# Moving four reloads behind semaphore waits, and five filler products to two, in a one-core transformer block

## The chip, the core and the metric

The kernel runs on one core of one Trainium2 chip. The metric is device time in microseconds (us), the median of several executions. All engines of the core work from their own instruction streams and meet through semaphores: PE (TensorE, matrix products), DVE (VectorE), ACT (ScalarE), POOL (GpSimd), and SP (SyncE), which issues nearly all DMA transfers of this kernel, in order.

## The reference

A block with adaptive layer norm, linear attention and a gated feed-forward network, on x of 2048 rows by 1024 columns in bf16. `phi(t)` is `t + 1` where t is positive and `exp(t)` elsewhere, plus 1e-6.

```python
mod = (silu(c) @ w_mod).reshape(1, 6, 1, -1)          # w_mod: 1024 x 6144
sa, ca, ga, sb, cb, gb = (mod[:, i] for i in range(6))

h = layernorm(x) * (1 + ca) + sa                      # x: 1 x 2048 x 1024
q, k, v = split_heads(h @ wqkv)                       # 32 heads of 32
pq, pk = phi(q), phi(k)
kv = einsum('bhsd,bhse->bhde', pk, v)
z  = sum over s of pk
o  = (pq @ kv) / (pq @ z + 1e-6)
x  = x + ga * (merge_heads(o) @ wo)

h = layernorm(x) * (1 + cb) + sb
x = x + gb * ((silu(h @ w_gate) * (h @ w_up)) @ w_down)   # 1024 -> 3584 -> 1024
```

## The kernel before

Every instruction is written out in Python in program order through a small recorder, `_Prog`. It notes which bytes of SBUF and which PSUM banks each operation reads and writes and derives the semaphore waits from that; each engine then gets its operations in the order in which they were recorded. Because of the recorder nearly all instructions bear one source line in the profile, L176, and are told apart by the names of their tiles. The order of the work is the order of the Python calls; there is no planner. `P.wait_for(engine, ops)` (line 195) records no operation, only a wait of that engine for the given ones.

SBUF is one arena with offsets given by hand, and tiles share places over time. Three places matter here. `XRES` holds x, 16 tiles of 128 rows (`st` 0 to 15); layer norm overwrites it in place, so x must be loaded a second time before the first residual addition. `STGX[0]` and `STGX[1]` (2 MB each) take column blocks of `w_mod`; both lie where `RB`, the reciprocals of the denominators, lay before. `AT`, used in the feed-forward part, lies over both later.

The stages, in order:

1. The start (lines 398 to 650). x tiles 0 to 3, then the `w_mod` columns of the first scale (`WCA`) and of the first shift (`WSA`), and `wqkv` are loaded on SP's queue. PE transposes the normalised x tiles and computes the scale as columns (`mod_sc(WCA, ...)`: weight load of a 128 x 128 piece of `WCA`, product with one column of `silu(c)`). Between them stand filler products, `warm(n)`: 128 x 128 by 128 x 512, with operands `IDENT` and `E1`, whose result in a PSUM bank is not read. Here are 13 before the transposes of tile 0, and more between these transposes and the first scale columns.
2. Products for q and k over four chunks of 512 rows (`q_phase_chunk0`, `k_group`, `chunk`). Side work such as layer norms and the multiply-accumulate of a `w_mod` block (`macc`, on DVE) is hung into them.
3. The loop over g (line 1005): 16 groups of 16 products, `pk` against the normalised x in `XRES`, giving G, from which kv follows as `WV^T G`, head by head. That last product is `kvt_mm(half)` (line 962), 128 small products of 32 columns. `m_mm(half, nh, banks)` (line 972) multiplies kv by `wo` in 16 products of 32 x 32 by 512 and copies four banks to `MW`, two with ACT and two with DVE.
4. Output of attention and residual (line 1083): for each `st` and each half `nh` of 512 columns `wo_part(st, nh, hgs)` (line 992) makes products of `PQT` with `MW`, and `wo_res(st, nh)` (line 998) adds the PSUM result to `XRES` on DVE. Four PSUM banks (`WO_BANKS`) are used in turn. For tiles 0 and 1 the first four of eight products of each half are done earlier, between `kvt_mm(1)` and `m_mm(1, ...)`; the rest follows in the order (0,0), (1,0) for st = 0 and (0,1), (1,1) for st = 1. The same loop holds the second layer norm of tiles 0 to 3 and `macc` with `STGX[0]`, whose result `MHL` is transposed by a DMA into `MHLT`.
5. Feed-forward over four chunks of 512 rows (line 1107), with weights streamed by `gu_load`. `macc` with `STGX[1]` is in its first chunk.

The reloads are issued on SP around the end of the g loop: `stgx1` (into `STGX[0]`) at g = 10; after the loop `stgx2` (into `STGX[1]`), then four reloads of 256 KB for tiles 0 to 3 of `XRES` (`xr0` to `xr3`), then, after the calls of `m_mm(1, 1, ...)`, three reloads of 1 MB for tiles 4 to 7, 8 to 11 and 12 to 15 (`xr4` to `xr6`). SP meets nothing but the waits of these transfers themselves: `stgx2` for the last reader of `RB`, the `XRES` reloads for PE's reads in the last group.

Of the kernel before, what the change touches and what calls it, by code (L numbers as in the profile page):

```python
# [9 lines left out]
ALU = mybir.AluOpType  # L10
# [252 lines left out]
def bass_adaLN_cond__linear_attn_block__swiglu_ffn__prompt_kernel(  # L263
# [16 lines left out]
    NCH = 4  # L280
# [5 lines left out]
    with ExitStack() as es:  # L286
# [6 lines left out]
        def T(name, off, shape, dt):  # L293
            n = 1
            for s_ in shape[1:]:
                n *= s_
            assert off % 32 == 0 and off + n * mybir.dt.size(dt) <= ARENA, (name, off, shape)
            return nc.alloc_sbuf_tensor_at(name, shape, dt, offset=base + off)

        KB = 1024  # L300
        XRES = T("xres", 0, [128, NST, D], BF16)
# [30 lines left out]
        SUMXH = T("sumxh", SM + 2816, [128, NST, 2], FP32)  # L332
# [17 lines left out]
        STGX = [T("stgx%d" % i, (72 + 16 * i) * KB, [128, NDT, D], BF16) for i in range(2)]  # L350
# [28 lines left out]
        PS = nc.alloc_psum_tensor("ps", [128, 8, 512], FP32)  # L379
# [5 lines left out]
        xv = A_x[0].rearrange("(t p) d -> p t d", p=128)  # L385
# [6 lines left out]
        wmv = w_mod.rearrange("(kt p) n -> p kt n", p=128)  # L392
        cv8 = c.rearrange("o (kt p) -> (o kt) p", p=128)

        P = _Prog()
# [57 lines left out]
        def warm(n=1, bank=2):  # L453
            for _ in range(n):
                P.pe("matmul", out=PS[:, bank, :], lhsT=IDENT[:], rhs=E1[:, 0, :], start=True, stop=True)
# [142 lines left out]
        def act_var(st):  # L598
            P.dve("scalar_tensor_tensor", out=MV[:, st, 1:2], in0=SUMX[:, st:st + 1], scalar=SUMX[:, st:st + 1],
                  in1=SUMSQ[:, st:st + 1], op0=ALU.mult, op1=ALU.subtract)  # L600
            P.dve("tensor_scalar", out=VE[:, st:st + 1], in0=MV[:, st, 1:2], scalar1=-1.0, scalar2=EPS, op0=ALU.mult,
                  op1=ALU.add)
# [7 lines left out]
        def tile_transposes(*js):  # L610
            for dt in range(NDT):
                for j in js:
                    c = (dt % 2) * 512 + j * 128
                    P.pe("transpose", out=PSB[:, 4 + dt // 2, c:c + 128], in_=XRES[:, j, dt * 128:(dt + 1) * 128],
                         identity=IDENT[:])
# [3 lines left out]
        for f in s0_:  # L619
# [3 lines left out]
        s2_[1]()  # L623
        act_xn(0, MV[:, 0, 0:1])
        tile_transposes(0)
        warm(5, bank=3)
        act_var(1)
        P.pool("tensor_tensor", out=RSTD[:, 1:2], in0=VE[:, 1:2], in1=NEGHALF[:, 0:1], op=ALU.pow)
        P.pool("tensor_scalar", out=NMR[:, 1:2], in0=SUMX[:, 1:2], scalar1=RSTD[:, 1:2], scalar2=-1.0,
               op0=ALU.mult, op1=ALU.mult)  # L630
# [80 lines left out]
        def macc(src, kt):  # L711
            if kt == 0:
                P.dve("tensor_scalar", out=ACC[:], in0=src[:, kt, :], scalar1=SILUF[:, kt:kt + 1], scalar2=None,
                      op0=ALU.mult)
            else:
                P.dve("scalar_tensor_tensor", out=ACC[:], in0=src[:, kt, :], scalar=SILUF[:, kt:kt + 1], in1=ACC[:],
                      op0=ALU.mult, op1=ALU.add)

        def macc_split():
            P.dve("tensor_copy", out=MHL[:, 0, :], in_=ACC[:])  # L720
            P.dve("tensor_tensor", out=MHL[:, 1, :], in0=ACC[:], in1=MHL[:, 0, :], op=ALU.subtract)
            xbar(MHLT[:], MHL[:].rearrange("p i d -> p (i d)"))

        def mod_red():
            P.dve("tensor_reduce", out=RED[:], in_=MHLT[:].rearrange("d (i m) p -> d m i p", i=2),
                  axis=mybir.AxisListType.XY, op=ALU.add)

        def mod_fin_col(idx, plus_one):
            P.dve("tensor_copy", out=MODTMP[:, 0:8], in_=RED[:])
            if plus_one:  # L730
                P.dve("tensor_scalar", out=MODTMP[:, 0:8], in0=MODTMP[:, 0:8], scalar1=1.0, scalar2=None,
                      op0=ALU.add)
            P.dve("tensor_copy", out=MODCOL[:, idx, :], in_=MODTMP[:, 0:8])
# [186 lines left out]
        def g_evac(g):  # L920
            h, dt = g // NDT, g % NDT
            bank = G_BANKS[1 if g == 14 else g % 5]
            i = g % 2
            P.act("activation", out=GTMP[:, i, :], in_=ZB[:, h * 512:(h + 1) * 512], func=ACT.Copy,
                  scale=MODCOL[:, 1, dt:dt + 1])
            P.dve("scalar_tensor_tensor", out=G[:, dt, h * 512:(h + 1) * 512], in0=PS[:, bank, :],
                  scalar=MODCOL[:, 0, dt:dt + 1], in1=GTMP[:, i, :], op0=ALU.mult, op1=ALU.add)
# [44 lines left out]
        def m_mm(half, nh, banks):  # L972
            for k in range(4):
                for g in range(4):
                    h = (g + k) % 4
                    P.pe("matmul", out=PS[32 * h:32 * h + 32, banks[g], :],
                         lhsT=KVT[32 * g:32 * g + 32, half, 32 * h:32 * h + 32],
                         rhs=WO[32 * g:32 * g + 32, 4 * half + h, nh * 512:(nh + 1) * 512], start=True, stop=True,
                         skip_group_check=True)
            for g in range(4):  # L980
                dst = MW[:, 4 * half + g, nh * 512:(nh + 1) * 512]
                if g % 2 == 0:
                    P.act("activation", out=dst, in_=PS[:, banks[g], :], func=ACT.Copy)
                else:
                    P.dve("tensor_copy", out=dst, in_=PS[:, banks[g], :])
# [6 lines left out]
        def wo_part(st, nh, hgs):  # L992
            bank = WO_BANKS[(2 * st + nh) % 4]
            for hg in hgs:
                P.pe("matmul", out=PS[:, bank, :], lhsT=PQT[:, hg, st * 128:(st + 1) * 128],
                     rhs=MW[:, hg, nh * 512:(nh + 1) * 512], start=(hg == 0), stop=(hg == NHG - 1))

        def wo_res(st, nh):
            bank = WO_BANKS[(2 * st + nh) % 4]
            xs = XRES[:, st, nh * 512:(nh + 1) * 512]  # L1000
            P.dve("scalar_tensor_tensor", out=xs, in0=PS[:, bank, :], scalar=1.0, in1=xs, op0=ALU.mult,
                  op1=ALU.add, accum_out=SUMXH[:, st, nh:nh + 1])

        ev = 0
        for g in range(16):
# [21 lines left out]
            if g == 10:  # L1027
                P.dma("stgx1", STGX[0][:], wmv[:, :, 3072:4096])
        g_evac(15)
        P.dma("stgx2", STGX[1][:], wmv[:, :, 5120:6144])  # L1030
        for st in range(4):
            P.dma("xr%d" % st, XRES[:, st, :], xv[:, st, :])
        wo_part(0, 0, range(4))
# [5 lines left out]
        wo_part(1, 0, range(1, 4))  # L1039
        wo_part(1, 1, range(4))  # L1040
        m_mm(1, 1, [4, 5, 7, 6])
        for ch in range(1, NCH):
            P.dma("xr%d" % (3 + ch), XRES[:, 4 * ch:4 * ch + 4, :], xv[:, 4 * ch:4 * ch + 4, :])

        def ln2_rstd(ch):
            sl = slice(4 * ch, 4 * ch + 4)
# [8 lines left out]
        def ln2_xn(st):  # L1055
            P.dve("tensor_scalar", out=XN2[:, :, st % 4, :], in0=XRES[:, st, :].rearrange("p (dt q) -> p dt q", q=128),
                  scalar1=MEAN2[:, st:st + 1], scalar2=RSTD2[:, st:st + 1], op0=ALU.subtract, op1=ALU.mult)

        def th2_dma():
            xbar(H2T[:].rearrange("p dt (j s) -> p (dt j) s", j=4), XN2[:].rearrange("p dt j q -> p (dt j q)"))  # L1060

        def th2_mod():
            for dt in range(NDT):
                P.pool("tensor_scalar", out=H2T[:, dt, :], in0=H2T[:, dt, :], scalar1=MODCOL[:, 2, dt:dt + 1],
                       scalar2=MODCOL[:, 3, dt:dt + 1], op0=ALU.mult, op1=ALU.add)

        def ln2_sq(st):
            P.act("activation", out=JUNK[:], in_=XRES[:, st, :], func=ACT.Square, accum_out=SUMSQ[:, st:st + 1])
            if st % 4 == 3:
                ln2_rstd(st // 4)  # L1070
# [12 lines left out]
        for st in range(NST):  # L1083
            for (sw, nh) in (((0, 0), (1, 0)), ((0, 1), (1, 1)))[st] if st < 2 else ((st, 0), (st, 1)):
                wo_part(sw, nh, range(4, 8) if st < 2 else range(8))
                wo_res(sw, nh)
            if st >= 1:
                ln2_sq(st - 1)
            for kt in ((), (0,), (1,), (2, 3), (4,), (5,), (6, 7))[st] if st < 7 else ():
                macc(STGX[0], kt)  # L1090
            if st == 6:
                macc_split()
            if st == 8:
                mod_red()
                mod_fin_col(3, False)
            if st == 7:
                for jj in range(4):
                    ln2_xn(jj)
                th2_dma()
            if st == 8:  # L1100
                th2_mod()
            if st == 7:
                for q in range(4):
                    gu_load(q)
        ln2_sq(NST - 1)
        out_ops = []
        for ch in range(NCH):
            nxt = ch + 1 if ch + 1 < NCH else None
            for ft in range(NFT):
# [27 lines left out]
                if nxt is None and ft in (8, 12):  # L1137
# [3 lines left out]
                          in1=GB_B[:, 896:1024].unsqueeze(1).to_broadcast([128, f1 - f0, 128]), op=ALU.mult)  # L1141
# [5 lines left out]
            for j in range(4):  # L1147
                st = 4 * ch + j
# [7 lines left out]
                for nh in range(2):  # L1156
                    i = nh
                    parts = [(0, 384, bb + 1), (384, 512, 4)] if last and nh == 1 else [(0, 512, bb + nh)]
                    for (c0, c1, pb) in parts:
# [5 lines left out]
                        xs = XRES[:, st, nh * 512 + c0:nh * 512 + c1]  # L1165
# [45 lines left out]
```

## Time and profile before

| what | value |
|---|---|
| median of 10 executions | 830.33 us (829.62 to 831.01) |
| profiled execution: own time | 829.62 us |
| profiled execution: span from first to last instruction | 827.9 us |
| PE busy | 816.5 us, 99% of the span |
| DVE, ACT, POOL busy | 310.6, 197.4, 40.6 us |
| granted TensorE clock | 1.000 |
| `xres` reloads of 1 MB, issue to landing | 13.6 us (median) |
| `out`, 128 KB, issue to landing | 1.7 us (median) |

The span leaves about 1.7 us of the execution's own time outside. A group line of the timeline gives start, time and count of like instructions, and in brackets how long the engine was idle before them and what ended it. "issue" stands where no semaphore explains the idle time. PEld are PE's weight loads, which run beside its products. In the DMA views q1 is the queue of ordinary transfers, q8 and q14 bring instructions.

### The profile page before, as it was taken

Reading aid. Unit: us, or ns where it says so; the run is one execution under the profiler, and the core shown is the slowest. Engines: PE = TensorE matmul, PEld = TensorE weight load, DVE = VectorE, ACT = ScalarE, POOL = GpSimd, SP = SyncE. Lnnn points to the kernel's source line nnn. Section 1 sums busy time; section 2 is a strip of 40 time slices with the busy share of each in tenths; the row PEclk is TensorE's granted clock in tenths of the full one; section 3 lists DMA queues with packets and bytes.
Section 4 is the critical chain, followed back from the end, with each engine's and each line's share of the span. In section 5 each row is a group of like instructions: output and inputs, shape, how many; then the busy total and the mean of one; then the engine's idle time right before and its main releaser. Section 6 shows DMA issues by size and latency. Waiting matters only on the chain.

```text
span 827.9 us, 10429 instructions
## 1 busy us (share of the span) xinstructions
PE 816.5 (99%) x4244; PEld 376.3 (45%) x4323; DVE 310.6 (38%) x664; ACT 197.4 (24%) x336; POOL 40.6 (5%) x59
## 2 busy tenths in 40 slices
PE   8999999999999999999999999999999999999998
PEld 4544444444444444444444444444444444444444
DVE  5797997476955521111221112122111111221111
ACT  4757643123242111011111101111110111111011
POOL 1010000000130000030000003000000300000000
DMA  9969656866397995700455571045557004553000
GB/s 319 289 151 231 149 159 158 183 185 257 68 261 229 290 253 155 181 27 20 129 151 151 154 178 32 19 125 156 151 152 187 26 16 127 152 152 89 0 26 26
DMA packets 199360, 119.32 MB, mean 144 GB/s; under 512 B 57992, under 2 KB 183056, under 8 KB 199312
## 3 DMA queue, kind: packets, MB, share of 16 engines
q1 hardware_dynamic: 199296, 118.65, 53.3%
q8 instruction: 34, 0.56, 0.3%
q14 instruction: 14, 0.11, 0.0%
q10 hardware_dynamic: 16, 0.00, 0.0%
HBM read 100.67 MB, written 4.33 MB: 127 GB/s over the span
## 4 chain that ended last, share of the span: by engine, by line
PE 97%; DVE 1%; issue 1%; DMA 0%; ACT 0%; DVEq 0%; ACTq 0%
PE ps L176 97%; DVE acc L176 1%; DVE pkt L176 0%; DMA cs<-in_c_dram 0%; DVE e L176 0%; DVE pqt L176 0%; ACT e L176 0%; DVE xres L176 0%; DVE ht L176 0%; DVEq L247 0%; ACTq L247 0%
## 5 line engine op out<-in xcount | busy, mean ns | idle before, releaser
L176 PE MATMUL ps<-h2t,gug 128*128 128x512 bf16 x878 | 210.1, 379 | 0.9
L176 PE MATMUL ps<-h2t,guu 128*128 128x512 bf16 x878 | 209.9, 379 | 0.9
L176 DVE TENSOR_TENSOR at<-sg,ps 128x512 bf16<-128x512 bf16 x112 | 77.0, 687 | 282.8 <-PE ps L176 270.6
L176 ACT ACTIVATE sg<-ps 128x512 bf16<-128x512 f32 x112 | 66.9, 597 | 309.7 <-PE ps L176 298.3
L176 PEld LDWEIGHTS ps<-h2t,guu 128*128 128x128 bf16 x896 | 87.7, 98 | 105.7
L176 PEld LDWEIGHTS ps<-h2t,gug 128*128 128x128 bf16 x896 | 87.6, 98 | 105.5
L176 PE MATMUL ps<-wd_a,at 128*128 128x512 bf16 (+1 forms) x502 | 111.9, 377 | 0.5
L176 PE MATMUL ps<-ht,wqk 128*128 128x512 bf16 x499 | 110.3, 379 | 1.0 <-issue 0.2
L176 PE MATMUL ps<-wd_b,at 128*128 128x512 bf16 (+1 forms) x377 | 84.6, 377 | 0.4
L176 PEld LDWEIGHTS ps<-wd_a,at 128*128 128x128 bf16 x512 | 50.1, 98 | 59.7
L176 DVE TENSOR_TENSOR ut<-att,gb_b 128x512 bf16<-128x512 bf16 (+1 forms) x32 | 13.7, 429 | 167.5 <-ACT att L176 167.5
L176 PEld LDWEIGHTS ps<-ht,wqk 128*128 128x128 bf16 x512 | 49.5, 98 | 58.8 <-DVE ht L176 0.4
L176 ACT ACTIVATE att<-ps 128x512 bf16<-128x512 f32 (+1 forms) x32 | 17.4, 591 | 182.1 <-PE ps L176 182.1
L176 PEld LDWEIGHTS ps<-wd_b,at 128*128 128x128 bf16 x384 | 37.6, 98 | 44.6
L176 PE MATMUL ps<-mw,pqt 128*128 128x512 bf16 x249 | 55.6, 379 | 1.9 <-issue 1.6
L176 PE MATMUL ps<-pk,xres 128*128 128x512 bf16 x250 | 55.4, 379 | 0.6 <-issue 0.5
L176 POOL TENSOR_SCALAR h2t<-h2t,modcol 128x512 bf16<-128x512 bf16 x32 | 26.3, 839 | 383.1 <-DMA h2t<-xn 383.1
L176 ACT ACTIVATE e<-ps 128x512 bf16<-128x512 f32 x56 | 33.2, 604 | 31.7 <-PE ps L176 20.7
L176 PEld LDWEIGHTS ps<-mw,pqt 128*128 128x128 bf16 x256 | 24.7, 98 | 31.8 <-issue 2.2
L176 PEld LDWEIGHTS ps<-pk,xres 128*128 128x128 bf16 x256 | 24.7, 98 | 30.0 <-issue 0.9
L176 ACT ACTIVATE junk<-xres 128x1024 bf16<-128x1024 bf16 x24 | 25.4, 1058 | 36.1 <-DVE xres L176 35.8
L176 DVE SCALAR_TENSOR_TENSOR xres<-ps,xres 128x512 bf16<-128x512 f32 x32 | 21.5, 689 | 13.4 <-PE ps L176 13.2
(107 smaller groups left out, 337.6 us busy)
## 6 DMA issues: line engine op xcount, KB each, us to landing
gug<-in_B_w_gate_dram SPq DMA_DIRECT2D x56, 512.0 KB, 3.9
guu<-in_B_w_up_dram SPq DMA_DIRECT2D x56, 512.0 KB, 5.2
xres<-in_A_x_dram SPq DMA_DIRECT2D x20, 256.0 KB, 7.6
rb<-recip_den SPq DMA_DIRECT2D x8, 512.0 KB, 11.5
stgx<-in_w_mod_dram SPq DMA_DIRECT2D x2, 2048.0 KB, 8.4
wd_a<-in_B_w_down_dram SPq DMA_DIRECT2D x4, 1024.0 KB, 7.3
out_dram<-xres SPq DMA_DIRECT2D x31, 128.0 KB, 1.7
xres<-in_A_x_dram SPq DMA_DIRECT2D x3, 1024.0 KB, 13.6
```

Of the source, the lines that this page charges most:

```text
L176: return getattr(e, method)(**kw)
```

## The change

Two things change. First, `warm(5)` ahead of the first scale columns becomes `warm(2)`. Second, four transfers are taken from their places at the end of the g loop and after `m_mm(1, 1, ...)` and issued within the loop over `st`: after the residuals recorded for st = 0, 1 and 2 SP waits for the last of them and issues `xr4`, `xr5` and `xr6` in turn, and after those of st = 3 `stgx2`. `wo_res` returns its operation so that SP can wait for it. On SP the order becomes `stgx1`, `xr0` to `xr3`, `xr4`, `xr5`, `xr6`, `stgx2`, then the transpose of `MHL` as before. On PE three products and their three weight loads leave the stream; DVE, ACT and POOL keep their instructions and order.

```diff
         tile_transposes(0)
-        warm(5, bank=3)
+        warm(2, bank=3)
         act_var(1)
...
         def wo_res(st, nh):
...
-            P.dve("scalar_tensor_tensor", out=xs, in0=PS[:, bank, :], scalar=1.0, in1=xs, op0=ALU.mult,
-                  op1=ALU.add, accum_out=SUMXH[:, st, nh:nh + 1])
+            return P.dve("scalar_tensor_tensor", out=xs, in0=PS[:, bank, :], scalar=1.0, in1=xs, op0=ALU.mult,
+                         op1=ALU.add, accum_out=SUMXH[:, st, nh:nh + 1])
...
         g_evac(15)
-        P.dma("stgx2", STGX[1][:], wmv[:, :, 5120:6144])
         for st in range(4):
             P.dma("xr%d" % st, XRES[:, st, :], xv[:, st, :])
...
         m_mm(1, 1, [4, 5, 7, 6])
-        for ch in range(1, NCH):
-            P.dma("xr%d" % (3 + ch), XRES[:, 4 * ch:4 * ch + 4, :], xv[:, 4 * ch:4 * ch + 4, :])
...
         for st in range(NST):
             for (sw, nh) in (((0, 0), (1, 0)), ((0, 1), (1, 1)))[st] if st < 2 else ((st, 0), (st, 1)):
                 wo_part(sw, nh, range(4, 8) if st < 2 else range(8))
-                wo_res(sw, nh)
+                done = wo_res(sw, nh)
+            if st < 4:
+                P.wait_for("sp", [done])
+                if st < 3:
+                    ch = st + 1
+                    P.dma("xr%d" % (3 + ch), XRES[:, 4 * ch:4 * ch + 4, :], xv[:, 4 * ch:4 * ch + 4, :])
+                else:
+                    P.dma("stgx2", STGX[1][:], wmv[:, :, 5120:6144])
```

## The prediction

> **What bounds the kernel now.** I read the page first: busy time, then the chain that ended last.
>
> ```profile
> span 827.9 us, 10429 instructions
> ...
> PE 816.5 (99%) x4244; PEld 376.3 (45%) x4323; DVE 310.6 (38%) x664; ACT 197.4 (24%) x336; POOL 40.6 (5%) x59
> ...
> PE 97%; DVE 1%; issue 1%; DMA 0%; ACT 0%; DVEq 0%; ACTq 0%
> ```
>
> PE is the bound. A change off PE can gain only where PE sits idle, so the second view is what PE waited for, over the whole span.
>
> ```profile
> PE ps L176 <- DMA cs<-in_c_dram: 2.9, 1, 2.9
> PE ps L176 <- issue: 2.4, 6, 1.5
> ```
>
> 2.9 us pass before the first product and are not touched. The rest is 2.4 us of "issue", which is idle time with no semaphore behind it, and 1.5 of it is one gap. The third view, PE's timeline near the reloads, shows where it lies.
>
> ```profile
> 187.44 1.20 PE L176 MATMUL ps<-g,wv 128*32 128x32 bf16 x128
> ...
> 191.66 1.04 PE L176 MATMUL ps<-mw,pqt 128*128 128x512 bf16 x4
> 194.17 1.02 PE L176 MATMUL ps<-mw,pqt 128*128 128x512 bf16 x4 [1.47 <-issue]
> ```
>
> The gap falls between the two halves of st = 0. Nothing waits on data: the MW tiles of that half were copied out by 191.2, and the trace has no wait on the stalled product. The 128 products of `kvt_mm(1)` took only 1.20 us, so PE ate its instruction stream very fast. The DMA views of 187.6:191.7 and of 191.7:192.8 say what came late.
>
> ```profile
> DMA packets 843, 1.58 MB, mean 386 GB/s; under 512 B 70, under 2 KB 70, under 8 KB 843
> ```
>
> ```profile
> DMA packets 213, 0.43 MB, mean 391 GB/s; under 512 B 10, under 2 KB 10, under 8 KB 212
> ...
> q8 instruction: 1, 0.02, 6.3%
> ```
>
> For 4.1 us the engines carry reloads alone, at 386 GB/s; then one 16,384-byte packet of queue 8 (start 191.71, 1.11 us long) brings instructions, and PE goes on 1.35 us after it ends. SP's timeline shows whose traffic it was: the w_mod load (stgx2) and seven XRES reloads, issued back to back.
>
> ```profile
> 169.94 12.41 SPq L176 DMA_DIRECT2D stgx<-in_w_mod_dram  x2
> 183.00 5.86 SPq L176 DMA_DIRECT2D xres<-in_A_x_dram  x7
> ```
>
> Was the packet late? I counted PE's instructions in the trace's records (two for each weight load, one for each semaphore instruction). Where the DMA engines are quiet (217.33, 354.03, 654.68, 764.11, 791.42), the packet starts 100 to 103 instructions ahead of a multiple of 256. For the packet at 191.71 that point was passed at 187.59, inside `kvt_mm(1)`: it came **4.12 us late**. Two fetches under the w_mod and rb transfers came 4.5 and 2.5 us late. What the gap cost is the distance between the starts of the products around it, 192.32 and 194.17, less the usual 0.216: **1.63 us**.
>
> [...] In the trace the first fillers start 0.427 us apart, later ones 0.216, changing near 8.2.
>
> **Part 1: the three fillers.** Three products at 0.216 from the warm row are 0.65 us of PE work. Are they on the path?
>
> ```profile
> 8.77 0.80 PEld L176 LDWEIGHTS ps<-e,ident 128*128 128x128 bf16 x5
> 9.89 0.47 PEld L176 LDWEIGHTS ps<-siluc,wca 128*128 128x128 bf16 x16 [0.33 <-DMA wca<-in_w_mod_dram]
> ```
>
> The first scale column's weight load waits for the wca load, whose last share landed at 9.85. The five fillers end their starts at 9.68, so PE would be ready at 9.90, just when wca is. With two it is ready at 9.25 and idles 0.65. **Gain 0 in this execution.** If wca landed early[...], it gains up to 0.65; I keep 0 and use the other end for the range. [...] A side effect: six instructions leave the stream, so the block boundary at the gap moves three products (0.65 us) later; alone this would cut the gap to about 0.98.
>
> **Part 2: the reloads.** No transfer is added: three XRES reloads of 1 MB and the 2 MB w_mod load move behind semaphore waits. In SP's order stgx2 moves past seven reloads; the others keep their places. Before the change 6 MB follow each other from about 184 to 202. After it only the four reloads of 256 KB stay there: their issues (183.00 to 184.9) are held by PE's reads of XRES, as before, and 1 MB at 386 GB/s is 2.7 us, so they are through by about 187.4. The fetch, due at 187.59, finds the engines empty. It may be 3.1 us late still, since PE runs dry at 192.54 (193.2 with part 1) and needs the packet 1.11 + 1.35 us earlier. So the gap goes: **-1.63 us**. What is next: the third half needs the last MW copy, done at 193.14 on DVE, and reaches it at 194.05; the next fetch is due near 191.3, before any moved reload is issued. From 194 on PE follows itself without a gap to the end, so the 1.63 stays.
>
> The waits cost nothing if the reloads still come in time. SP waits for DVE's second residual of each st. Without the gap, the one of st 0 ends near 194.5 (193.06 + two of 0.77). I price a landing from the first w_mod load, 2 MB alone, 9.0 us from issue: 1 MB less at 0.41 MB/us gives 6.4. Tiles 4 to 7 are there at 201; DVE took up st 4's first residual at 207.00 before, 205.4 after. **Slack 4.4 us**, and PE has three more PSUM banks. The next reloads are issued near 196.0 and 199.5 and needed after 215; stgx2 near 202.9, landing by 212, first read near 245. Behind SP's last wait stands the MHLT transpose, issued at 219.46 before: no other queue waits. Each wait instruction costs SP about 0.02 us.
>
> **Sum.** 0 - 1.63: span 827.9 to 826.3, and this execution's own 829.62 to 828.0. It was the fastest of the ten; the median is 0.71 above. Taken off the median, 1.63 gives 828.7. A median run's gap is hardly smaller than the fastest run's; I put a quarter of the 0.71 down to it, so -1.8: **828.5 us**.
>
> **The rivals.** 0.2% of this kernel, 1.66 us, is about what a measurement can tell from no change.
> - *The gap goes, start unchanged* (my forecast): 0.77; its own range 827.9 to 829.0. It sits on the 1.66 bound: 0.50 beyond, 0.27 within.
> - *The start gains as well* (wca early): 828.7 - 0.65 = 828.05; 0.07. Against it: the landing at 9.85 above.
> - *The fetch stays late*, because the four small reloads still stand in front or its lag isn't traffic; only part 1's shift remains: -0.65, 829.7; 0.06. For it: one lag of 2.5 us at only 186 GB/s; against it: that lag still meets the 3.1.
> - *The clock falls back.* Between 8.4 and 12.4 PE has little but short products, and three long ones leave. [...] Chance 0.06 (0.04 slower). Against it: the 1.47 us gap at 192.7 left the clock full, PEclk 1.00.
> - *The reload comes too late*: PE stops once tile 4 lands after about 208.3 (four banks full) and is slower over the bound from 211.6, 17 us after issue. The page's 13.6 for such a load was behind 3 MB of others. Chance 0.04, 832.
>
> Faster 0.57; same 0.27 + 0.06 + 0.02 = 0.35; slower 0.08. The range 827.4 to 830.4 takes in the first three cases[...].
>
> **What would show it.** Right: no idle above 0.3 us in PE's timeline from 188 to 197; the queue 8 packet near 187.7 to 188.5, under light traffic; XRES reloads issued near 194.5, 196 and 199.5, stgx2 near 203; the first wca column still at 9.9 with PE idle 0.65 before it. Wrong: the gap with its packet near 191; products 0.427 apart after 12.4; a residual of st 4 waiting on the reload.

## The result and the profile after

| | before | after |
|---|---|---|
| median, compared on one chip | 830.41 us (52 executions) | 828.58 us (15 executions) |
| ratio | | 0.9975, 95% interval 0.9969 to 0.9982 |
| profiled execution: own time, span | 829.62, 827.9 us | 828.61, 826.8 us |

The change makes the kernel 1.83 us faster by the medians. The profiled executions differ by only 1.0 us: the one of before was the fastest of its ten, the one of after lies at its median.

First PE's waits over the whole span of the kernel after (what it waited for: us in total, times, longest).

```profile
PE ps L176 <- DMA cs<-in_c_dram: 2.9, 1, 2.9
PE ps L176 <- ACT xres L176: 1.1, 1, 1.1
PE ps L176 <- issue: 0.9, 5, 0.2
PE ps L176 <- DMA wca<-in_w_mod_dram: 0.4, 1, 0.4
```

"issue" fell from 2.4 us with one piece of 1.5 to 0.9 us with none above 0.2. What is new, ACT xres and wca, lies at the start. PE's timeline around the old gap (start, length, count):

```profile
188.03 1.19 PE L176 MATMUL ps<-g,wv 128*32 128x32 bf16 x128
189.39 0.59 PE L176 MATMUL ps<-mw,pqt 128*128 128x512 bf16 x2 [0.16 <-issue]
...
191.90 0.43 PE L176 MATMUL ps<-wo,kvt 32*32 32x512 bf16 x16
192.26 7.94 PE L176 MATMUL ps<-mw,pqt 128*128 128x512 bf16 x35
```

After the second `m_mm` the products of `MW` follow each other for 7.94 us; before, they broke off after four. The DMA view of the stretch 189.6:190.8 shows the instruction packet:

```profile
DMA packets 1, 0.02 MB, mean 14 GB/s; under 512 B 0, under 2 KB 0, under 8 KB 0
...
q8 instruction: 1, 0.02, 4.9%
```

It started at 189.67 and had the engines to itself. SP's timeline shows the reloads apart:

```profile
183.60 16.87 SPq L176 DMA_DIRECT2D xres<-in_A_x_dram  x7
203.56 0.37 SPq L176 DMA_DIRECT2D stgx<-in_w_mod_dram  x1
```

Seven reloads now take 16.87 us on SP instead of 5.86. The four moved transfers were issued at 195.00, 196.65, 200.11 and 203.56 and landed at 200.42, 204.28, 207.25 and 214.86.

Lined up weight load by weight load from the end, PE of after runs 0.38 us *behind* before at 12.4, 0.60 behind from 46 to 192, and 1.03 ahead from 200 to the end. So the gap gave exactly the 1.63 us, and this execution had lost 0.60 by 46, at waits for loads.

### The profile page after: what moved, and what is told of

Read it like the earlier page. It is cut to its first block, busy times and chain, and to the rows that moved or that the text cites. A ratio compares the mean times of both kernels' runs of the same rounds, so it can differ in the third digit from the quotient of the medians.

```text
span 826.8 us, 10422 instructions
## 1 busy us (share of the span) xinstructions
PE 815.4 (99%) x4241; PEld 375.8 (45%) x4320; DVE 311.3 (38%) x664; ACT 197.2 (24%) x336; POOL 40.8 (5%) x59
## 4 chain that ended last, share of the span: by engine, by line
PE 96%; DVE 1%; DMA 1%; issue 1%; SPq 0%; ACT 0%; DVEq 0%; ACTq 0%
PE ps L176 96%; DMA wca<-in_w_mod_dram 1%; DVE acc L176 1%; DVE pkt L176 0%; SPq L176 0%; DVE e L176 0%; DVE pqt L176 0%; ACT e L176 0%; DVE xres L176 0%; DVE ht L176 0%; DVEq L247 0%; ACTq L247 0%
```

## The experiments

Each is compared with the kernel before, run beside it on the same chip; there were three such groups, so kernels of different groups are best compared by their ratios. "Lost" is the step between the starts of the products around the gap less 0.216. PE's instructions are counted as in the prediction.

**Two fillers alone.** `warm(5)` to `warm(2)` in the kernel before.

```diff
-        warm(5, bank=3)
+        warm(2, bank=3)
```

> Two fillers instead of five, all reloads in their old places. Theory (late instruction fetch): the start gains nothing, since the first scale columns wait for wca (landing near 9.9 to 10.2); but the stream is 6 instructions shorter, so PE runs dry 3 products later and the gap near 192.7 shrinks from 1.63 to about 0.98 us: 0.65 faster than before, about 829.8 us. Rival A (the fillers were on the path at the start): 0.65 more, about 829.1, with the first wca column at 9.25. Rival B (only the reloads matter, the block boundary does not): no change, 830.4.

Measured: 829.57 us, ratio 0.9992 (0.9985 to 0.9998), or 0.66 us by the ratio. PE's timeline:

```profile
10.61 0.55 PE L176 MATMUL ps<-siluc,wca 128*128 128x1 bf16 x16 [0.70 <-DMA wca<-in_w_mod_dram]
...
192.00 0.43 PE L176 MATMUL ps<-wo,kvt 32*32 32x512 bf16 x16
192.37 1.69 PE L176 MATMUL ps<-mw,pqt 128*128 128x512 bf16 x7
195.18 2.10 PE L176 MATMUL ps<-mw,pqt 128*128 128x512 bf16 x8 [1.12 <-issue]
```

At the start PE waits 0.70 for wca, about the length of the three fillers. The gap comes after seven products instead of four: three later, as six fewer instructions demand, and it costs 1.28 us instead of 1.63. The fillers act 180 us after the place where they stand. The count of products is the evidence here, not the time: the gap accounts for 0.35 of the 0.66 us, and the interval of the ratio reaches from 0.17 to 1.25 us, so that the median fell on the forecast 0.65 is partly luck.

**The reloads alone.** The change with `warm(5)`.

> Reloads late as in the change, five fillers kept. Theory: the fetch comes before PE runs dry with or without the fillers, so this alone gives all of the change's gain: about 1.8 faster than before, 828.6 us, no gap between 188 and 197. Rival (the two parts add up): about 1.2 faster only, 829.2 us, the rest belonging to the fillers.

Measured: 828.32 us, ratio 0.9977 (0.9969 to 0.9986), no gap:

```profile
192.12 5.14 PE L176 MATMUL ps<-mw,pqt 128*128 128x512 bf16 x22
```

The whole gain of the change is here; the parts do not add up.

**Half of the reloads.** Only stgx2 moved behind st = 3 (first), or only the three XRES reloads moved behind st = 0 to 2 (second), each with five fillers.

> Only the 2 MB w_mod load stgx2 is moved behind st = 3; the three 1 MB reloads of XRES stay where they were; five fillers. Theory: 4 MB still follow each other from about 184 to 195 at 390 GB/s, so the fetch due at 187.6 is again about 4 us late and the gap stays at 1.4 to 1.7 us: no change, 830.2 to 830.5. Rival (it is the 2 MB load in front, or the place in the queue, that counts): all or most of the 1.8 us gained, 828.6 to 829.

> Only the three 1 MB reloads of XRES are moved behind st = 0 to 2; the 2 MB w_mod load stays in its old place; five fillers. Theory: 3 MB follow each other from about 184 to 192, the fetch due at 187.6 meets full traffic, is about 4 us late (packet near 191.5), the gap stays: 830.2 to 830.5. Rival (only what is queued after the fetch is due delays it): gap gone, 828.6 to 829.

Measured: 830.66 us, ratio 1.0000 (0.9990 to 1.0009), and 829.91 us, ratio 0.9993 (0.9985 to 1.0002). These medians lie 0.2 above and 0.3 below the forecast range, but the gap stands in both. For the second, PE's timeline:

```profile
192.55 1.04 PE L176 MATMUL ps<-mw,pqt 128*128 128x512 bf16 x4
195.09 2.10 PE L176 MATMUL ps<-mw,pqt 128*128 128x512 bf16 x8 [1.50 <-issue]
```

The fetch was 4.55 and 4.03 us late, the gap cost 1.94 and 1.67 us. Either half leaves 3 or 4 MB in the stretch in which the fetch is due. The small gain by the second's median isn't clear of noise, and its profile doesn't show one at the gap.

**Traffic put back.** The late reloads with five fillers, and two needless loads of 2 MB.

```diff
         g_evac(15)
+        P.dma("stgd0", STGX[1][:], wmv[:, :, 5120:6144])
         for st in range(4):
             P.dma("xr%d" % st, XRES[:, st, :], xv[:, st, :])
+        P.dma("stgd1", STGX[1][:], wmv[:, :, 5120:6144])
```

> The late reloads with five fillers (as in e2_reloads), plus traffic that is not needed: the 2 MB w_mod block is loaded into STGX[1] twice more, once ahead of and once behind the four small XRES reloads, so that 5 MB follow each other from about 184 to 197 as before. Theory (traffic delays the instruction fetch): fetch about 4 us late again, gap of 1.4 to 1.8 us back near 193, about 830.2 us. Rival (the gain comes from the order or the waits on SP, not from quiet engines): stays at 828.3.

Measured: 829.97 us, ratio 0.9993 (0.9985 to 1.0001). The second extra load had to wait for the first and was issued only at 190.67, yet the stretch 188.5:192.3 is full and PE stops again:

```profile
DMA packets 782, 1.47 MB, mean 387 GB/s; under 512 B 64, under 2 KB 64, under 8 KB 782
```

```profile
192.53 1.04 PE L176 MATMUL ps<-mw,pqt 128*128 128x512 bf16 x4
194.97 2.32 PE L176 MATMUL ps<-mw,pqt 128*128 128x512 bf16 x10 [1.40 <-issue]
```

The needed reloads keep the order and the SP waits of the 828.3 us kernel; the two extra loads alone bring the gap back.

The five kernels with a gap, side by side:

| kernel | fetch late, us | PE's instructions when it stops | from packet's end to next product, us | lost, us |
|---|---|---|---|---|
| before | 4.12 | 2753 | 1.36 | 1.63 |
| two fillers alone | 4.34 | 2753 | 1.41 | 1.28 |
| w_mod load alone | 4.55 | 2753 | 1.36 | 1.94 |
| XRES reloads alone | 4.03 | 2753 | 1.48 | 1.67 |
| traffic put back | 3.94 | 2753 | 1.47 | 1.56 |

All five stop at the same instruction of the stream, although in the second it belongs to a product three places further on, and all go on about 1.4 us after the packet. The trace of before has one packet for every 256 instructions of PE: 22 packets after the one at 217.33 (count 2969) up to 819.10 (count 8601). This is what shows that PE ran out of instructions.

**The boundary shifted, traffic kept.** The kernel before with ten fillers instead of 13, and none instead of five.

> All reloads in their old places; ten fillers instead of 13 at the start and none instead of five ahead of the scale columns. Theory (PE runs dry at the block boundary): the stream is 16 instructions shorter, PE runs dry eight products or 1.73 us later, so a fetch 4.1 to 4.4 us late leaves a gap of 0 to 0.3 us although the traffic is the same: 828.7 to 829.0 us. The start gains nothing (it waits for x tile 0 and wca). Rival (the traffic disturbs PE at this place whatever the boundary): gap stays at 1.5, about 830.4. [...]

Measured: 831.06 us, ratio 1.0009 (1.0002 to 1.0016): slower, for another reason than the gap. PE's timeline and the stretches (length, busy time of PE, PEld, DVE, ACT, POOL, then PEclk, DMA share, GB/s):

```profile
13.99 0.61 PE L176 MATMUL ps<-siluc,wca 128*128 128x1 bf16 x16
14.47 5.81 PE L176 MATMUL ps<-ht,wqk 128*128 128x512 bf16 x20
...
195.59 6.65 PE L176 MATMUL ps<-mw,pqt 128*128 128x512 bf16 x29
```

```profile
11.00:14.00 3.00, 2.97 (x41) 2.97 (x42) 0.48 (x2) 0.00 (x0) 0.00 (x0) 0.50 1.09 366
14.00:18.00 4.00, 4.00 (x29) 1.82 (x28) 2.10 (x6) 2.52 (x3) 0.00 (x0) 0.60 1.08 360
...
191.60:195.80 4.20, 4.20 (x163) 2.06 (x147) 1.60 (x4) 1.14 (x3) 0.00 (x0) 1.00 1.06 388
```

Of the gap 0.22 us is left (forecast 0 to 0.3), under 388 GB/s and with a fetch 4.21 us late: lateness alone does little harm when PE has eight products more. What is left falls at instruction 2753 once more, now after twelve products instead of four, 1.48 us after the packet's end. The weight loads show it:

```profile
198.41 1.61 PEld L176 LDWEIGHTS ps<-mw,pqt 128*128 128x128 bf16 x8 [0.34 <-issue]
```

So the forecast holds at the gap. It failed for the time, 828.7 to 829.0 us, and that is explained in part only. In the profiled execution PE was 1.14 us behind the kernel before at the first scale column, since wca landed later. Then PEclk was at one half for about 6.8 us (0.90 in 8:11, 0.50 in 11:14, 0.60 in 14:18; so from 10.4 to 17.2, if it read 1.00 around that), and PE was 3.58 behind after it. The gap gave back 1.42, and the span ended 3.0 us longer. Over all 21 executions the mean clock was below 1.000 in 15, but the six at 1.000 took 830.92 to 831.35 us, and those at 0.998 only 829.80 to 830.88. The figure cannot settle this: in the profile of before it reads 1.00 in 3.0:6.9, where the fillers start 0.427 us apart, twice the 0.216 of later ones. The ten of this kernel start 0.427 us apart, too. The six may have had more products at that distance; no profile of such an execution was kept, and this stays open.

**The first wca load split.** The change, and the change with five fillers, with columns 0 to 255 loaded first.

```diff
-        ca_load(0)
+        for a_, b_ in ((0, 256), (256, 512)):
+            P.dma("wca0_%d" % a_, WCA[:, :, a_:b_], wmv[:, :, D + a_:D + b_])
```

> The change, with the first wca load split into two of 512 KB, columns 0 to 255 first (the two that the first scale columns need). Theory (the start waits for the wca landing, which hid the fillers): the first half lands about 1.4 us earlier, the first wca column starts near 9.3 instead of 10.3, and PE then waits for the normalised tile 3 on DVE: 0.3 to 0.5 us faster than the change, about 828.1. Rival (the start is bound elsewhere): 828.5.

> As e8_split, but with five fillers. Theory: now the fillers end after the landing and are on the path: the first wca column starts near 9.9 to 10.1, so this is 0.3 to 0.6 us slower than e8_split, near e2_reloads at 828.3 to 828.5. Rival (fillers never on the path): same as e8_split.

Measured: 828.46 and 828.62 us, both 0.9979 (0.9971 to 0.9987): no gain over the unsplit kernels that can be measured, and no difference of 0.3 to 0.6 us between the two. The first scale columns did start earlier, at 9.69 and 9.88 against 10.28 and 10.36 in the profiles of the change and of the reloads alone. For the kernel with five fillers the waits in 42:46.5 show where a lead can go:

```profile
DVE ht L176 <- DMA ht<-xres: 1.9, 1, 1.9
PEld ps L176 <- DVE ht L176: 1.5, 7, 0.2
```

Lined up by weight loads, it was 0.49 us ahead of the reloads alone (the same kernel with the wca load whole) at 36, and level with it at 46. There PE meets the rows that SP transposes by DMA and DVE then scales, and waits for them piece by piece. Not every pair of profiles shows this. Against a second profile of that kernel, with five fillers in the next group, the lead fell between 36 and 46 from 1.13 to 0.55 only; and with two fillers the lead over the change was 0.59 at the first scale column, 0.06 at 36 and 0.26 from 46 on. Where PE meets the loads of the first 46 us differs by some tenths from execution to execution.

**None, two and five fillers, late reloads.**

> The change with no filler at all ahead of the first scale columns (the 13 at the start stay). Theory (fillers covered by the wca landing and again by the transposed rows near 43 to 45 us): 828.3 to 828.7 as with two or five, as long as the array keeps full clock. Rival (fillers hold the clock): in part of the runs the mean clock falls to 0.998 or 0.996 and 1.3 to 3 us are lost, the median near 829.5 or above.

> The change as it is, two fillers, for a comparison on one chip with none and five. Theory: 828.3 to 828.7, no difference from five fillers that can be measured. Rival (two fillers gain at the start): 0.3 to 0.65 below five fillers.

> Late reloads with five fillers, again, beside two and none on one chip. Theory: 828.3 to 828.7. Rival (two fillers gain at the start): 0.3 to 0.65 above two fillers, near 829.

Measured: none 829.56 us, ratio 0.9988 (0.9981 to 0.9994); two 828.35, 0.9976 (0.9967 to 0.9986); five 828.48, 0.9977 (0.9968 to 0.9987). Two and five are alike. With two, PE's timeline reads

```profile
8.49 0.59 PE L176 MATMUL ps<-e,ident 128*128 128x512 bf16 x2
10.55 0.55 PE L176 MATMUL ps<-siluc,wca 128*128 128x1 bf16 x16 [1.47 <-DMA wca<-in_w_mod_dram]
```

so PE waits. Without fillers the clock fell to a mean of 0.998 in 9 of 21 executions, 829.65 to 830.51 us with a median of 829.90; the other twelve have one of 828.72. With two fillers it fell in none of these ten, and in 3 of 61 over all kernels with two (two of them of the change itself, 829.88 and 829.94). With five it fell in 8 of 207, 6 of these 8 in the kernel before. In the comparison of the change the clocks of the kernel before are not on record; nine of its 52 executions took 831.97 us or more, which in the three later groups only its executions at 0.998 did. So the rival is real, and two fillers keep it about as rare as five, as far as these counts go.

## Why the prediction was right

- *The gap is a late instruction fetch, and traffic makes it late.* Shown: by the stop at instruction 2753 in all five and, shifted, in the sixth, by the traffic put back, and by the shifted boundary. Why traffic delays the packet this much is not shown: the 843 packets in the 4.1 us ahead of it took 0.08 us each on their engines (mean), so one of them in front explains far less than the lag.
- *The gap goes whole, -1.63.* Right: PE of after gains 1.63 on before at that place and keeps it to the end. The median fell by 1.83, close to the 1.8 forecast, but that closeness is luck: a quarter of 0.71 was added because a median execution's gap might be larger. The gaps in the profiles where the boundary is unmoved are 1.56 to 1.94, too few to show it.
- *The fetch finds the engines empty at 187.59.* The size was off twice. The four small reloads had landed at 189.27, not 187.4: the stretch 188.2:189.7 still carried 86 GB/s on average. And the packet came 1.47 us late, not near zero, and 1.06 to 1.23 in the other six kernels with late reloads and no extra traffic. In the split load with two fillers the engines moved nothing in 187.9:189.0, and the packet still came 1.06 after the mark. My estimate is that the mark hides a delay: it came from places where PE takes 0.216 us for two instructions, and 1 us is some ten of them; in `kvt_mm(1)`, where 128 products and their weight loads take 1.19 us, it is some two hundred. That the delay is the same in both places was not shown. By this estimate about 1 us of the 4.12 is there without traffic, and about 3 is traffic. The allowance of 3.1 us was large enough for both. One reading was too generous without harm: without the gap PE reaches the third half at 193.40, not 194.05, so the last `MW` copy was 0.26 us ahead, not 0.91 (after: copy done at 193.74, half begun at 194.00).
- *The start gains nothing.* Right, by wca (waits of 0.36 to 1.47 us with two fillers). What I missed is that PE meets further loads behind it, at 43 to 46 us above all, so that my second case (wca early, 0.65 more) is less likely than it looked: the split load made wca early and gave nothing that can be measured.
- *Fillers alone shrink the gap to 0.98.* Three products later was exact; 1.28 was lost. Of the 0.30 between, 0.22 is a fetch later by that much in this execution.
- *The waits cost nothing.* Right. Tiles 4 to 7 landed at 200.42 (forecast 201), DVE took up the first residual of st 4 at 205.97, and in 187:246 no engine waits for an XRES reload. stgx2 took 11.3 us, not 9, far ahead of its reader.
- *The fetch stays late.* Refuted for the full change, and true for each half of it.
- *The clock falls back.* With two fillers the mean clock was lowered in 3 of 61 executions, with none in 9 of 21, so my 0.06 was for a real case. Taking fillers away brought it: PEclk was at one half for about 6.8 us in the profile with ten fillers and none, and in the kernel without the later fillers the executions with a lowered mean clock have a median 1.2 us above that of the others. What in PE's work decides on it, and how much of it is too little, was not shown.

## What to carry to other kernels

Idle time that no semaphore explains, shortly after a run of very small instructions (here 128 products in 1.20 us), is worth checking against the packets of the instruction queue: count instructions up to the stop and see whether it stays the same when the program shifts, as it did here at 2753. With a late fetch as the cause, all of the bulk traffic had to leave the stretch between the burst and the boundary here; with half of it moved the gap still cost 1.94 and 1.67 us. And before pricing work taken from a start, look for the next places where the engine meets a load: a lead can end there, as 0.49 us did here between 36 and 46.

## What was not expected of the hardware

The instruction packet came about 4 us late (3.94 to 4.55) in all six profiles with reloads around it, whether the traffic behind it ended soon (XRES reloads alone, where 58 GB/s were left in 192.5:193.6) or went on (before, to 202). The lag does not follow the rate: it was longest, 4.55, with the w_mod load alone late, where the engines moved 328 GB/s in 188.9:193.6, against 385 to 388 in the other five. The fetch after it, due at 191.30 in the kernel before, even came 6.65 us late, at 197.95; it did no harm: at one packet for 256 instructions PE needed it, as I estimate, only 256 instructions after the first stop, at about 221. After a late packet PE always took another 1.36 to 1.48 us. And a few fillers of 0.216 us each made a difference to the clock: with two, 8.5 to 10 us into the span, its mean stayed at 1.000 in 58 of 61 executions, with none in 12 of 21.
